# A fused attention, expert and SoLU kernel: conversions in chunks of 512 columns, and a compaction by 32 slots

## The chip, the cores and the metric

The kernel runs on one core of a Trainium2 chip. The metric is the device time of one execution in microseconds. The profile is one execution taken by the hardware profiler. Five engines run side by side, each with its own instruction queue in order: PE (matrix products; PEld is its weight load), DVE (vector), ACT (scalar, activations), POOL (vector work and indirect DMAs) and SP (it only issues DMAs).

## The reference

Three layers follow each other. The experts' layer needs a selection that is worked out from the first layer's output, and the last layer's two weight matrices come as float64.

```python
# 1 local attention: chunks of 32 queries, 16 left, 8 right, 8 memory keys
scores = scale * (q_c @ k_full.T); a = softmax(scores); out = a @ v_full
x = out.reshape(3072, 512)
# 2 experts, each takes 384 tokens; pairs are taken in order of logit
logits = x @ w_gate                       # 3072 x 8
for idx in np.argsort(-logits.flatten()):
    tok, e = idx // 8, idx % 8
    if assigned[tok] >= 0 or counts[e] >= 384: continue
    assigned[tok] = e; counts[e] += 1
x[mask_e] = np.maximum(x[mask_e] @ w1[e], 0) @ w2[e]
# 3 SoLU: w_in 512 x 1024 and w_out 1024 x 512 are float64
h = x @ w_in
solu = h * softmax(h)
ln = (solu - mean) / sqrt(var + 1e-6) * g_ln
return ln @ w_out
```

## The kernel before, in words

**Attention** (`attention`, from line 61) works through 24 blocks of 128 tokens. For one block the tiles are `kd`, `qt`, `vd` (inputs), `s` (scores), `p` (softmax), `t`/`pt` (transposed), `o`, and `xs` (the block's output, also written to `x_dram`). `xtp`, `xt`, `g` and `L` are the transposed output and the gate's logits. SP's queue issues all input loads in the order of the program.

**Route** (line 520) finds in eight rounds which expert is full next and which 384 tokens it takes. A round is a search for a threshold (tiles `ge`, `some`, `sat`, `base`), a prefix sum that gives each taken token a slot (`sl`, with `s` as the 0/1 mark of being taken), and `compact` (line 762), which turns slots into a list of tokens `idx` of 128 partitions x 3. It does so by one-hot matrices and matmuls: `ohl` is a one-hot of the slot's low bits, `rhs` holds, by the slot's high bits, the token's number, and the PE product `r` sums it up in the slots' order. Round 0 runs before the first expert, round r+1 beside stage r; it then removes the taken tokens (`gone`, `left`, `el`, `L`) and begins the next search.

**Experts** (line 806) has eight stages. A stage is `g12` (two products of 96 matmuls 128x384 each: `h` from `xh`, `xl` and `w1h`, `w1l`, then `y` from `hh`, `hl` and `w2h`, `w2l`) and two kinds of units: `g3` (`h2 = y . in`, 24 matmuls 128x512 for each of three token tiles) and `g4` (`o = l . out`, as many, for the stage before). All products are of three terms: every operand is split in a high and a low part. The tokens' rows are gathered on POOL (`xg<-x_dram,idx`), transposed on PE (`tp`) and split (`xh` on ACT, `xl` on DVE); the weights come as `raw<-in_w_dram,iw` on POOL and are split too (`w1h` on ACT, `w1l` on DVE). Results leave by an indirect DMA on POOL (`out_dram<-ob,idx`).

**Fixed** (line 410) turns the float64 matrices `win` and `wout` into pairs `in_h`, `in_l` and `out_h`, `out_l`, in chunks of `CHUNK` columns, beside all this. One chunk (line 442) is a load `raw` on SP, `v<-raw` on ACT, then on DVE the sign `e<-raw`, `v<-v,e`, the exponent `e<-v`, and `e<-raw,e`; then one or two additions on POOL, `in_h` or `out_h` on ACT, and `in_l` on POOL or `out_l` mostly on DVE. Fourteen of `win`'s 16 chunks are converted beside the attention, `wout`'s beside stages 0 and 1.

**The order.** Every instruction goes through `Timed` (line 386), and so all rows of the profile carry line 398; work is told apart by the names of tiles. `Pace` (line 238) keeps a modelled clock per engine. Jobs (generators) stand beside the main program; at each `tick` a job whose rank is within `limit` and whose condition is met emits its next instructions. Conversions have rank 3 and are spaced by `EVERY_A` and `EVERY_OUT`; where a matmul needs a chunk that is not yet there, `need` (line 506) ticks until it is. All this happens when the program is built; on the chip each engine runs its queue in the order so written:

```python
            if job[2] <= self.limit and job[0] <= self.now and (
                    job[1] is None or self.clk[job[1]] <= (self.now + self.rush if self.late() else
                                                         min(self.now + self.spare, self.soon()))):
```

## Time and profile before

| | us |
|---|---|
| median of 3 runs | 793.64 |
| the runs | 793.40, 793.64, 796.08 |
| profiled execution, its own time | 792.05 |
| its span | 790.3 |
| PE busy (share of the span) | 717.0 (91%) |
| DVE busy | 550.4 (70%) |
| ACT busy | 340.9 (43%) |
| POOL busy | 207.4 (26%) |

The span is the time from the first to the last instruction that the profiler saw; the profiled execution's own time is 1.75 us longer. PE is busy nine tenths of the span, and so time can be lost or won in two kinds of place: where PE has no work to do, and where PE's own work grows or shrinks. Along the span the attention part ends at about 117 us, the selection of round 0 at 145 us, and the first expert's matmuls begin at 153.28 us.

### The profile page before, as it was taken

Reading aid. Unit: us, or ns where it says so; the run is one execution under the profiler, and the core shown is the slowest. Engines: PE = TensorE matmul, PEld = TensorE weight load, DVE = VectorE, ACT = ScalarE, POOL = GpSimd, SP = SyncE. Lnnn points to the kernel's source line nnn. Section 1 sums busy time; section 2 is a strip of 40 time slices with the busy share of each in tenths; the row PEclk is TensorE's granted clock in tenths of the full one; section 3 lists DMA queues with packets and bytes.
Section 4 is the critical chain, followed back from the end, with each engine's and each line's share of the span. In section 5 each row is a group of like instructions: output and inputs, shape, how many; then the busy total and the mean of one; then the engine's idle time right before and its main releaser. Section 6 shows DMA issues by size and latency. Waiting matters only on the chain.

```text
span 790.3 us, 14784 instructions
## 1 busy us (share of the span) xinstructions
PE 717.0 (91%) x5728; PEld 619.6 (78%) x5728; DVE 550.4 (70%) x1536; ACT 340.9 (43%) x680; POOL 207.4 (26%) x288
## 2 busy tenths in 40 slices
PE   6988963699999949999999999999999999999993
PEld 5766653688789737998899889888988898899883
DVE  7787967699999974993798389838973952563150
ACT  1566630243574443431653174227324642463170
POOL 4344520631621342003300520052014211400121
PEclk7999995699999978999999999999999999999997
DMA  7999891720620340102600340053006110600100
GB/s 248 336 331 337 292 349 56 231 85 29 219 87 27 100 141 30 64 1 81 213 0 1 128 165 1 1 177 118 1 14 210 70 41 27 209 19 0 41 15 27
DMA packets 32326, 89.37 MB, mean 113 GB/s; under 512 B 4480, under 2 KB 4608, under 8 KB 32256
## 3 DMA queue, kind: packets, MB, share of 16 engines
q0 software_dynamic: 13056, 46.14, 17.2%
q1 hardware_dynamic: 19200, 42.29, 15.6%
q8 instruction: 45, 0.74, 0.4%
q14 instruction: 25, 0.20, 0.1%
HBM read 75.83 MB, written 12.58 MB: 112 GB/s over the span
## 4 chain that ended last, share of the span: by engine, by line
PE 69%; DVE 19%; issue 4%; POOL 3%; ACT 2%; DMA 2%; POOLq 0%; DVEq 0%
PE h L398 30%; PE y L398 17%; PE o L398 15%; DVE e L398 4%; PE tp L398 4%; PE r L398 3%; DVE sum L398 2%; DVE p L398 2%; DVE mx L398 2%; DVE v L398 1%; DMA xg<-x_dram,idx 1%; ACT p L398 1%; DVE ge L398 1%; DVE nm L398 1%; DMA raw<-in_win_dram 1%
## 5 line engine op out<-in xcount | busy, mean ns | idle before, releaser
L398 PE MATMUL y<-hh,w2h 128*128 128x384 f32 x256 | 91.7, 358 | 5.4 <-DVE e L398 5.4
L398 POOL DMA_INDIRECT out_dram<-ob,idx x24 | 26.1, 1089 | 265.6 <-ACT ob L398 223.4
L398 PE MATMUL y<-hl,w2h 128*128 128x384 f32 x256 | 88.9, 347 | 0.1
L398 PE MATMUL o<-out_h,lh 128*128 128x512 f32 x192 | 78.4, 409 | 11.2 <-ACT out_h L398 11.2
L398 PE MATMUL y<-hh,w2l 128*128 128x384 f32 x256 | 87.4, 341 | 0.0
L398 POOL DMA_INDIRECT raw<-in_w_dram,iw x64 | 62.6, 978 | 73.4 <-DVE w1l L398 27.9
L398 PE MATMUL o<-out_l,lh 128*128 128x512 f32 x192 | 76.6, 399 | 1.2 <-DVE out_l L398 1.2
L398 PE MATMUL h<-in_h,yh 128*128 128x512 f32 x192 | 76.7, 399 | 0.0
L398 PE MATMUL h<-in_l,yh 128*128 128x512 f32 x192 | 76.4, 398 | 0.0
L398 PE MATMUL o<-out_h,ll 128*128 128x512 f32 x192 | 76.4, 398 | 0.0
L398 DVE TENSOR_REDUCE nm<-h 128x1 f32<-128x512 f32 x48 | 33.0, 688 | 61.9 <-PE h L398 61.5
L398 PE MATMUL h<-in_h,yl 128*128 128x512 f32 x192 | 75.8, 395 | 0.0
L398 ACT ACTIVATE hh<-h 128x384 fp32r<-128x384 f32 x64 | 31.4, 490 | 81.0 <-PE h L398 71.2
L398 PE MATMUL h<-xh,w1h 128*128 128x384 f32 x256 | 58.3, 344 | 0.7 <-ACT xh L398 0.7
L398 ACT CAST w2h<-raw 128x512 fp32r<-128x512 f32 x64 | 39.5, 619 | 44.8 <-PE y L398 44.8
L398 PE MATMUL h<-xh,w1l 128*128 128x384 f32 x256 | 58.7, 346 | 0.0
L398 PE MATMUL h<-xl,w1h 128*128 128x384 f32 x256 | 56.9, 343 | 0.0
L398 PEld LDWEIGHTS y<-hh,w2h 128*128 128x128 f32 x256 | 48.2, 188 | 7.2 <-DVE e L398 6.8
L398 DVE TENSOR_TENSOR xl<-tp,xh 128x512 fp32r<-128x512 f32 x24 | 16.6, 691 | 50.0 <-ACT xh L398 50.0
L398 PEld LDWEIGHTS o<-out_h,lh 128*128 128x128 f32 x192 | 36.7, 191 | 18.5 <-ACT out_h L398 11.9
L398 ACT ACTIVATE ob<-o,k 128x512 f32<-128x512 f32 x24 | 16.5, 688 | 79.5 <-PE o L398 76.8
L398 DVE TENSOR_TENSOR w2l<-raw,w2h 128x512 fp32r<-128x512 f32 x64 | 44.3, 694 | 7.8 <-ACT w2h L398 7.8
(192 smaller groups left out, 1694.1 us busy)
## 6 DMA issues: line engine op xcount, KB each, us to landing
vd<-in_vx_dram SPq DMA_DIRECT2D x48, 256.0 KB, 4.9
kd<-in_kx_dram SPq DMA_DIRECT2D x48, 176.0 KB, 4.8
qt<-in_q_dram SPq DMA_DIRECT2D x24, 256.0 KB, 4.7
x_dram<-xs SPq DMA_DIRECT2D x6, 1024.0 KB, 10.4
raw<-in_win_dram SPq DMA_DIRECT2D x16, 256.0 KB, 5.0
raw<-in_wout_dram SPq DMA_DIRECT2D x16, 256.0 KB, 2.7
raw<-in_w_dram,iw POOLq DMA_INDIRECT x64, 5.5
xg<-x_dram,idx POOLq DMA_INDIRECT x24, 3.7
```

The lines of the kernel that those rows point to most:

```text
L398: return fn(*args, **kw)
```

## The change

- Conversions go in chunks of 512 columns, half as many; the intervals in `EVERY_A`, `EVERY_OUT` and `DUE_OUT` are doubled, and `raw`, `v`, `e` have two buffers each, not three. The sign is read from the dense `v` that ACT wrote, not from every second word of `raw`, so it now waits for ACT.
- From the end of round 0's searches until the first expert's rows are split, jobs of rank 3 are held (`limit = 2`). The first split of `w1` for the first expert is written after the gather.
- `compact` takes the slot as 32a+b: a one-hot of b with 32 columns (two pieces of 128x384 where there were four of 128x768), `rhs` with 12 columns for a and for each of two numbers, and 24 matmuls in which four column tiles of PE take turns. The result is cast to `cc`, four more matmuls with `rep` sum the four tiles and place them on partitions, and `tok` and `idx` follow.
- `junk` shares a ring with the output tile `ob`; some constants share work tiles.

```diff
...
-EVERY_OUT = 3.5
+EVERY_OUT = 7.0
-CHUNKS_A = 14
+CHUNKS_A = 7
-EVERY_A = 4.4
+EVERY_A = 8.8
-DUE_OUT = 5.42
+DUE_OUT = 10.84
...
-    CHUNK = 256
+    CHUNK = 512
...
-            yield from self.take("raw", 3)
+            yield from self.take("raw", 2)
             while self.hold:
                 yield 0.0
-            r = self.tmp.tile([128, C, 2], I32, tag="raw", name="raw", bufs=3)
+            r = self.tmp.tile([128, C, 2], I32, tag="raw", name="raw", bufs=2)
...
-            yield from self.take("v", 3)
-            v = self.tmp.tile([128, C], F32, tag="v", name="v", bufs=3)
-            e = self.tmp.tile([128, C], F32, tag="e", name="e", bufs=3)
+            yield from self.take("v", 2)
+            v = self.tmp.tile([128, C], F32, tag="v", name="v", bufs=2)
+            e = self.tmp.tile([128, C], F32, tag="e", name="e", bufs=2)
             vi, ei, top = v.bitcast(I32), e.bitcast(I32), r[:, :, 1]
             nc.scalar.activation(v, top.bitcast(F32), AF.Copy, scale=2.0 ** -112)
+            yield "act"
             yield "spare", "dve"
-            V.tensor_scalar(ei, top, -0x80000000, None, op0=ALU.bitwise_and)
-            yield "act"
+            V.tensor_scalar(ei, vi, -0x80000000, None, op0=ALU.bitwise_and)
             yield "spare", "dve"
             V.scalar_tensor_tensor(vi, vi, 3, ei, op0=ALU.logical_shift_left, op1=ALU.bitwise_or)
...
+        self.col = col
+        self.cnum = iota(k.tile([128, NT], F32, name="cnum"), [[1, NT]], 0, 0)
+        self.atab = iota(k.tile([128, CAP // 32], F32, name="atab"), [[32, CAP // 32]], 32, 0)
+        self.rep = k.tile([128, 32], BF, name="rep")
+        with nc.allow_low_precision(reason="0 or 1"):
+            V.tensor_reduce(self.rep, ident.rearrange("p (j b) -> p b j", b=32), axis=AX.X, op=ALU.add)
...
                 yield from self.search(lo, oh, zero, r, r + .5)
+                if not r:
+                    self.beside.limit = 2
...
-        V.tensor_scalar(low, sl, 127, None, op0=ALU.bitwise_and)
-        b = self.t("b", [NT, TT])
-        V.tensor_scalar(b[:, :, 2], sl, 256.0, None, op0=ALU.is_ge)
-        V.tensor_scalar(b[:, :, 0], sl, 128.0, None, op0=ALU.is_lt)
-        yield "spare", "dve"
-        cc = self.t("cc", [2 * TT])
-        rhs = self.t("rhs", [NT, 2, TT], BF)
-        half, part = NT // 2, NT // 4
-        for c0 in (0, half):
-            ohl = []
-            for c1 in (c0, c0 + part):
-                o = self.w.tile([128, part, 128], BF, tag="ohl", name="ohl", bufs=2)
-                V.tensor_tensor(o, self.row[:, None, :].to_broadcast([128, part, 128]),
-                                low[:, c1:c1 + part, None].to_broadcast([128, part, 128]), op=ALU.is_equal)
-                ohl.append(o)
-                if c1 == 0:
-                    V.scalar_tensor_tensor(b[:, :, 1], b[:, :, 0], -1.0, b[:, :, 2], op0=ALU.mult, op1=ALU.subtract)
-                    V.tensor_scalar(b[:, :, 1], b[:, :, 1], 1.0, None, op0=ALU.add)
-                    V.tensor_tensor(b, b, s1[:, :, None].to_broadcast([128, NT, TT]), op=ALU.mult)
-                    for a in range(2):
-                        V.tensor_tensor(rhs[:, :, a], b, self.cp[:, :, a:a + 1].to_broadcast([128, NT, TT]),
-                                        op=ALU.mult)
-                yield 0.0
+        V.tensor_scalar(low, sl, 31, None, op0=ALU.bitwise_and)
+        am = self.t("am", [NT])
+        V.scalar_tensor_tensor(am, sl, 32.0, low, op0=ALU.add, op1=ALU.subtract)
+        V.tensor_tensor(am, am, s1, op=ALU.mult)
+        yield idle
+        rhs = self.t("rhs", [NT, 2, A], BF)
+        V.tensor_tensor(rhs[:, :, 1], self.atab[:, None, :].to_broadcast([128, NT, A]),
+                        am[:, :, None].to_broadcast([128, NT, A]), op=ALU.is_equal)
+        yield idle
+        V.tensor_tensor(rhs[:, :, 0], rhs[:, :, 1], self.cnum[:, :, None].to_broadcast([128, NT, A]), op=ALU.mult)
+        yield idle
+        V.tensor_scalar(rhs[:, :, 1], rhs[:, :, 1], self.col, None, op0=ALU.mult)
+        ohl, part = [], NT // 2
+        for c in (0, part):
+            yield idle
+            o = self.w.tile([128, part, 32], BF, tag="ohl", name="ohl", bufs=2)
+            V.tensor_tensor(o, self.row[:, None, 0:32].to_broadcast([128, part, 32]),
+                            low[:, c:c + part, None].to_broadcast([128, part, 32]), op=ALU.is_equal)
+            ohl.append(o)
+        if r:
             yield "dve"
-            p = yield from self.take()
-            for c in range(half):
-                T.matmul(p[:, 0:2 * TT], ohl[c // part][:, c % part],
-                         rhs[:, c0 + c].rearrange("p a t -> p (a t)"), start=c == 0, stop=c == half - 1)
-            yield "pe"
-            if c0 == 0:
-                V.tensor_copy(cc, p[:, 0:2 * TT])
-            else:
-                V.tensor_tensor(cc, cc, p[:, 0:2 * TT], op=ALU.add)
-            self.held = False
+        p = yield from self.take()
+        for c in range(NT):
+            j = c % 4
+            T.matmul(p[32 * j:32 * j + 32, 0:2 * A], ohl[c // part][:, c % part],
+                     rhs[:, c].rearrange("p w a -> p (w a)"), start=c < 4, stop=c >= NT - 4,
+                     tile_position=(0, 32 * j), skip_group_check=True)
+        yield "pe"
+        cc = self.t("cc", [2, TT, 4], BF)
+        V.tensor_copy(cc.rearrange("p w t j -> p (w t j)"), p[:, 0:2 * A])
+        self.held = False
+        yield "dve"
+        p = yield from self.take()
+        for j in range(4):
+            T.matmul(p[32 * j:32 * j + 32, 0:2 * TT], self.rep, cc[:, :, :, j], start=True, stop=True,
+                     tile_position=(0, 32 * j), skip_group_check=True)
+        yield "pe"
+        tok = self.t("tok", [TT])
+        V.tensor_scalar(tok, p[:, 0:TT], 128.0, None, op0=ALU.mult)
         idx = self.k.tile([128, TT], I32, name=f"idx{r}")
-        V.scalar_tensor_tensor(idx, cc[:, 0:TT], 128.0, cc[:, TT:2 * TT], op0=ALU.mult, op1=ALU.add)
+        V.tensor_tensor(idx, tok, p[:, TT:2 * TT], op=ALU.add)
...
-                self.fixed.need(0, self.beside, {4 * dt + 2 * half, 4 * dt + 2 * half + 1})
+                self.fixed.need(0, self.beside, {2 * dt + half})
...
-        junk = self.wk.tile([128, DFF], BF, tag="junk", name="junk", bufs=1)
-        A.activation(junk, e, AF.Square, accum_out=sq[:, t:t + 1])
+        junk = self.wk.tile([128, DM], F32, tag="ob", name="junk", bufs=2)
+        A.activation(junk.bitcast(BF), e, AF.Square, accum_out=sq[:, t:t + 1])
...
-            self.fixed.need(1, self.beside, {2 * f, 2 * f + 1})
+            self.fixed.need(1, self.beside, {f})
...
-        self.beside.add(self.fixed.all(0, self.beside, 1.0, CHUNKS_A, 16))
+        self.beside.add(self.fixed.all(0, self.beside, 1.0, CHUNKS_A, 8))
         while 0 not in self.iw:
             tick()
         self.load_w(0, range(2))
-        self.split_w(0, 0, (1,))
         self.fixed.hold = True
         while 0 not in self.idx:
             tick()
...
         self.gather(0)
         self.load_w(0, (2,))
         self.fixed.hold = False
-        self.split_w(0, 1, (1,))
+        for f in range(2):
+            self.split_w(0, f, (1,))
...
-        self.beside.add(self.fixed.all(1, self.beside, EVERY_OUT, 0, 16))
+        self.beside.add(self.fixed.all(1, self.beside, EVERY_OUT, 0, 8))
         start = self.beside.now
-        self.beside.late = lambda: 16 - len(self.fixed.left[1]) < (self.beside.now - start - DUE_FROM) / DUE_OUT - 1
+        self.beside.late = lambda: 8 - len(self.fixed.left[1]) < (self.beside.now - start - DUE_FROM) / DUE_OUT - 0.5
...
```

The changed order, at the two places that matter below. First POOL in stage 1, where the rows of `x` for round 2 are gathered (`xg`), before the change; `v<-v,e` and `out_l` are steps of `wout`'s chunks, `na` to `k` are a norm of the last layer, and `raw` is a load of expert weights:

```order
99 L398 DMA raw_4299<-in_w_dram,iw_4188 128x1024
100 L398 DMA xg<-x_dram,idx_4370 128x512 x3
101 L398 TENSOR_TENSOR na<-s 128x3
102 L398 TENSOR_SCALAR na<-na 128x3
103 L398 TENSOR_TENSOR nv<-na 128x3
104 L398 TENSOR_TENSOR nv<-nv,q 128x3
105 L398 TENSOR_SCALAR nv<-nv 128x3
106 L398 TENSOR_TENSOR k<-nv,power 128x3
107 L398 TENSOR_TENSOR v<-v,e 128x256 x3
108 L398 TENSOR_TENSOR out_l<-v,out_h 128x256
109 L398 TENSOR_TENSOR v<-v,e 128x256
```

and POOL at the same place after it:

```order
73 L398 TENSOR_TENSOR k<-nv,power 128x3
74 L398 TENSOR_TENSOR v<-v,e 128x512 x2
75 L398 DMA raw_4127<-in_w_dram,iw_4029 128x1024
76 L398 DMA raw_4129<-in_w_dram,iw_4029 128x1024
77 L398 DMA raw_4131<-in_w_dram,iw_4029 128x1024
78 L398 DMA raw_4133<-in_w_dram,iw_4029 128x1024
79 L398 DMA raw_4135<-in_w_dram,iw_4029 128x1024
80 L398 DMA raw_4137<-in_w_dram,iw_4029 128x1024
81 L398 DMA xg<-x_dram,idx_4209 128x512 x3
82 L398 MEMSET spacer 1x1
83 L398 DMA out_dram<-ob,idx_2415 3072x512
```

Four additions of chunks stood behind the gather, the first three right behind the norm; now the last two stand ahead of the weight loads and the gather, and none comes after.

Second, DVE from the compaction of round 0 to the first expert, before:

```order
281 L398 TENSOR_TENSOR ohl<-row,low 128x768 x2
282 L398 TENSOR_TENSOR w1l<-raw_2421,w1h 128x512
283 L398 TENSOR_TENSOR cc<-cc,r 128x6
284 L398 SCALAR_TENSOR_TENSOR idx_2510<-cc 128x3
285 L398 SCALAR_TENSOR_TENSOR v<-v,e 128x256
286 L398 TENSOR_SCALAR e<-raw 128x256
287 L398 TENSOR_TENSOR xl<-tp,xh 128x4x128 x3
288 L398 TENSOR_TENSOR w1l<-raw_2421,w1h 128x512
289 L398 TENSOR_TENSOR w2l<-raw_2423,w2h 128x512 x2
290 L398 TENSOR_SCALAR gone<-s_2447 128x24
291 L398 TENSOR_TENSOR left<-left,es 128x8
```

and after, where the rows left out between go on from `gone` in the order of the kernel before:

```order
254 L398 TENSOR_TENSOR ohl<-row,low 128x384 x2
255 L398 CAST cc<-r 128x24
256 L398 TENSOR_SCALAR tok<-r 128x3
257 L398 TENSOR_TENSOR idx_2415<-tok,r 128x3
258 L398 TENSOR_TENSOR xl<-tp,xh 128x4x128 x3
...
266 L398 TENSOR_SCALAR ki<-m 128x24
267 L398 TENSOR_TENSOR ki<-ki,m 128x24
268 L398 SCALAR_TENSOR_TENSOR ge<-ki,zero,jtab 128x360
269 L398 TENSOR_TENSOR w1l<-raw_2342,w1h 128x512 x2
270 L398 TENSOR_TENSOR w2l<-raw_2344,w2h 128x512 x2
```

The first expert's `w1l` and `w2l` stood ahead of the removal of the taken tokens; now they stand behind it and behind the first comparison `ge` of the next search. No step of a conversion stands between any more.

## Rows read from the trace of the kernel before

**Rows 1.** Page, the chain that ended last: shares of the span by engine.
```profile
PE 69%; DVE 19%; issue 4%; POOL 3%; ACT 2%; DMA 2%; POOLq 0%; DVEq 0%
```

**Rows 2.** Windows: us, busy (count) PE PEld DVE ACT POOL, PEclk, DMA share, GB/s.
```profile
0.00:100.77 100.77, 83.95 (x1761) 65.10 (x1762) 81.36 (x190) 53.35 (x109) 45.78 (x60) 0.95 0.89 306
259.60:313.22 53.62, 41.23 (x189) 31.19 (x189) 37.99 (x116) 22.05 (x46) 19.05 (x27) 0.84 0.29 99
428.67:464.14 35.47, 35.47 (x181) 28.57 (x181) 19.16 (x53) 11.65 (x23) 14.31 (x16) 1.00 0.40 140
283.64:303.58 19.94, 8.56 (x23) 6.10 (x23) 10.32 (x31) 6.99 (x13) 9.76 (x17) 0.57 0.17 54
```

**Rows 3.** Timeline, PE in stage 1: start, us, work, idle before and releaser.
```profile
293.32 0.80 PE L398 MATMUL o<-out_h,lh 128*128 128x512 f32 x1 [9.60 <-ACT out_h L398]
...
297.94 0.80 PE L398 MATMUL o<-out_h,lh 128*128 128x512 f32 x1 [1.57 <-ACT out_h L398]
```

**Rows 4.** Timeline, POOL in the same stretch.
```profile
285.02 0.96 POOL L398 DMA_INDIRECT xg<-x_dram,idx  x1 [6.75 <-DVE L L398]
...
291.07 2.13 POOL L398 TENSOR_TENSOR v<-v,e 128x256 f32<-128x256 f32 x3
```

**Rows 5.** Groups of DVE by form: busy us, mean ns, idle before.
```profile
L398 DVE SCALAR_TENSOR_TENSOR e<-h,e 128x512 f32<-128x512 f32 x48 | 31.8, 688 | 7.5 <-ACT e L398 7.5
...
L398 DVE SCALAR_TENSOR_TENSOR e<-raw,e 128x256 f32<-128x256 uint32 x32 | 16.4, 511 | 0.5
L398 DVE SCALAR_TENSOR_TENSOR v<-v,e 128x256 int32<-128x256 int32 x32 | 16.3, 514 | 0.1
...
L398 DVE TENSOR_SCALAR e<-raw 128x256 int32<-128x256 int32 x32 | 13.3, 441 | 5.4 <-DMA raw<-in_win_dram 2.8 <-POOL v L398 2.6
...
L398 DVE TENSOR_SCALAR e<-v 128x256 int32<-128x256 int32 x32 | 10.5, 328 | 0.4
```

**Rows 6.** Timeline, DVE, a chunk step in stage 1.
```profile
286.46 0.43 DVE L398 SCALAR_TENSOR_TENSOR e<-raw,e 128x256 f32<-128x256 uint32 x1
```

**Rows 7.** Timeline, DVE, a chunk step of the attention part.
```profile
74.48 0.29 DVE L398 TENSOR_SCALAR e<-raw 128x256 int32<-128x256 int32 x1 [2.76 <-DMA raw<-in_win_dram]
```

**Rows 8.** Timeline, end of the attention part, PE and then DVE.
```profile
110.11 0.66 PE L398 MATMUL xtp<-ident,xs 128*128 128x128 f32 x4
...
112.66 0.68 DVE L398 COPY xt<-xtp 128x512 f32<-128x512 f32 x1
```

**Rows 9.** Timeline, DVE, compaction of round 0 and the selection behind it.
```profile
137.88 0.18 DVE L398 TENSOR_SCALAR low<-sl 128x24 int32<-128x24 int32 x1
...
138.21 0.94 DVE L398 TENSOR_TENSOR ohl<-row,low 128x768 bf16<-128x768 bf16 x1
...
145.44 0.16 DVE L398 SCALAR_TENSOR_TENSOR idx<-cc 128x3 int32<-128x3 f32 x1
...
155.67 0.30 DVE L398 TENSOR_SCALAR gone<-s 128x24 f32<-128x24 f32 x1
...
157.88 0.59 DVE L398 SCALAR_TENSOR_TENSOR ge<-ki,zero,jtab 128x360 bf16<-128x360 uint16 x1
```

**Rows 10.** Timeline, PE, the first expert's second group of matmuls.
```profile
154.66 1.48 PE L398 MATMUL h<-xh,w1l 128*128 128x384 f32 x4
```

**Rows 11.** Timeline, PE, transposes and compaction matmuls, each with its follower.
```profile
95.91 0.66 PE L398 MATMUL t<-ident,p 128*128 128x128 f32 x4
96.50 0.75 PE L398 MATMUL o<-vd,pt 128*32 128x128 f32 x20
...
196.01 0.46 PE L398 MATMUL r<-rhs,ohl 128*128 128x6 bf16 x12
196.33 0.42 PE L398 MATMUL y<-hl,w2h 128*128 128x384 f32 x1
...
753.32 0.60 PE L398 MATMUL tp<-ident,e 128*128 128x128 f32 x4
753.68 0.48 PE L398 MATMUL h<-in_h,yh 128*128 128x512 f32 x1
```

More of the change, by code (lines that the diff above doesn't have):

```diff
@@ L309, in cost @@
             return n / (480 if op == "tensor_tensor" else 960) + 0.15
-        t = (0.108 if op == "transpose" else 0.06 * n / 128 if kw.get("tile_position") else
+        t = (0.108 if op == "transpose" else max(0.03, 0.06 * n / 128) if kw.get("tile_position") else
              max(0.025, n / 2400 + 0.003))
@@ L473, in chunk @@
         else:
-            yield from self.take("v", 3)
-            v = self.tmp.tile([128, C], F32, tag="v", name="v", bufs=3)
+            yield from self.take("v", 2)
+            v = self.tmp.tile([128, C], F32, tag="v", name="v", bufs=2)
             nc.sync.dma_start(v, src[:, n * C:n * C + C])
@@ L532, in __init__, with consts @@
         self.held, self.stage = False, 0
-    def consts(self):
+    def consts(self, ident):
         nc, k = self.nc, self.k
@@ L551, in consts @@
             V.tensor_scalar(self.jtab[:, i], self.jtab[:, 3], float(16 ** (3 - i)), None, op0=ALU.mult)
-        off = iota(self.t("off", [8, E]), [[-15, 8], [0, E]], 0, 1)
+        off = iota(self.w.tile([128, 8, E], F32, tag="oh", name="off"), [[-15, 8], [0, E]], 0, 1)
         self.own = k.tile([128, 8, E], F16, name="own")
-        up = self.t("up", [8, E])
+        up = self.w.tile([128, 8, E], F32, tag="rhs", name="up")
         V.tensor_scalar(up, off, 0.0, None, op0=ALU.is_ge)
@@ L765, in compact @@
         V, T = nc.vector, nc.tensor
+        A, idle = CAP // 32, ("spare", "dve") if r else 0.0
         low = self.t("low", [NT], I32)
-        V.tensor_scalar(low, sl, 127, None, op0=ALU.bitwise_and)
-        b = self.t("b", [NT, TT])
-        V.tensor_scalar(b[:, :, 2], sl, 256.0, None, op0=ALU.is_ge)
-        V.tensor_scalar(b[:, :, 0], sl, 128.0, None, op0=ALU.is_lt)
-        yield "spare", "dve"
-        cc = self.t("cc", [2 * TT])
-        rhs = self.t("rhs", [NT, 2, TT], BF)
-        half, part = NT // 2, NT // 4
@@ L803, in compact @@
+        self.held = False
         self.idx[r] = idx
@@ L1191, in step @@
         beside.tick()
-    attention(nc, tc, q, kx, vx, wg, ident, x_dram, L, route.consts, step)
+    attention(nc, tc, q, kx, vx, wg, ident, x_dram, L, lambda: route.consts(ident), step)
     route.open_psum(ctx)
```

5 lines of the change are left out of this document (1 added, 4 removed).

## The prediction

> **What bounds the kernel now.** I read the chain of waits first: it gives 69% of the span to PE and 19% to DVE, 3% to POOL and 2% to DMA [rows 1]. So time is mostly PE's own work, and the second candidate is DVE where PE waits for it. Then I put stages side by side with the windows. The last part of stage 1, from the first `h2` matmul to the next stage's first `h`, takes 53.62 us, and the same 144 matmuls in stage 3 take 35.47 with PE busy all the time [rows 2]. Stage 1 thus loses 53.62 - 35.47 = 18.15 us. The reader is to see where: in 283.64 to 303.58 PE is busy for 8.56 us only, and the granted clock has a mean of 0.57 [rows 2]. PE's timeline names the wait: 9.60 us for `out_h`, and 1.57 for it again a little later [rows 3]. ACT's copy to `out_h` needs `v<-v,e` of POOL, and POOL's timeline shows why that is late: POOL waited 6.75 us for the selection with its gather of `x` for round 2 at 285.02, and three additions of chunks, queued behind it and behind a norm, began at 291.07 [rows 4]. The third place is the front. In the first 100.77 us DVE is busy for 81.36 us and the DMA engines for a share of 0.89 [rows 2]; one chunk step there waited 2.76 us for `raw` [rows 7].
>
> All sums below are made on the profiled execution's 792.05 us (span 790.3). The median of the runs shown, 793.64, is 1.59 us above it.
>
> **Stage 1's stall: -15.5 us.** In the new order of POOL the last two additions of `wout`'s chunks stand ahead of the weight loads and the gather, so no matmul `o` can wait for the selection through them. What goes: 9.60 + 1.57 us of idle PE, and the low clock. The 8.56 us of PE work in that window ran at about half speed, so half of it, 4.3 us, comes back. 9.60 + 1.57 + 4.3 = 15.5. Bounds: 9.6 (the one wait alone) and 18.2 (all that stage 1 loses). What is late next is the gathered `x` itself: stage 1 would now end at 313.2 - 15.5 = 297.7 us, and the gather's three issues would still be out by about 289 (285.02 and three times 0.96 with small gaps), so its rows have some 9 us to land, be transposed and split. I take it as enough; a rival below does not.
>
> **Attention: -3.2 us.** Two chunks of 256 columns become one of 512. Four DVE steps each: 511 + 514 + 441 + 328 ns = 1.79 us per chunk now, 14 chunks in this part, so 25.1 of DVE's 81.4 busy us [rows 2, 5]. A step with fixed time f costs 0.43 us at 256 columns [rows 6] and 0.688 at 512 (the same kind of operation, `e<-h,e`) [rows 5], so f = 2 x 0.43 - 0.69 = 0.17 us is saved once per pair: 4 steps x 7 pairs x 0.17 = 4.8 us. The sign from the dense tile costs 0.328 where the strided read cost 0.441: 14 x 0.11 = 1.6 us. Together 6.4 us of DVE. How much of it is on the path? DMA moves the same bytes at a share of 0.89, so at one end nothing is gained; at the other all 6.4, since the chain has 19% on DVE and 2% on DMA. I take the middle, 3.2. The sign now waits for ACT; other DVE work stands between, so I cost it at nothing; without that cover it is one ACT copy per chunk. With two `raw` buffers a load is issued only when the chunk before last is through with its last DVE step; its cost is the slower rival.
>
> **End of the attention part: -1.8 us.** The last-but-one transposes `xtp` ended at 110.11 + 0.66 = 110.77, and DVE's copy `xt` began at 112.66, with steps of chunks queued ahead of it [rows 8]. In the new order none is: 112.66 - 110.77 = 1.9, less 0.1 for the signal, 1.8. Bounds 0 (something else late there, as the last `o`) and 4 (each of the two last copies gains as much).
>
> **Compaction of round 0: -3.1 us.** Only here does PE wait for it. Before: 137.88 to 145.44 + 0.16, 7.7 us [rows 9]. After: three short steps at 0.18 = 0.5; three steps for `rhs` on 288 columns, the nearest row being `ge` with 0.59 us for 360 columns, so 0.47 each = 1.4; two one-hots of half of the old one's 768 columns, 0.94 / 2 = 0.5 each, 1.0; `cc`, `tok` and `idx` at 0.16 = 0.5; and two trips to PE and back at an estimated 0.6 = 1.2. Sum 4.6, gain 3.1; bounds 2.5 (the `rhs` steps at 0.69 like a step of 512 columns) and 4.5 (the trips at 0.2 each and `rhs` at 0.3).
>
> **First expert's weights: +2.8 us.** What the front gains there is given back by the order on DVE: `w1l` now stands behind `gone` to `ge`. These run from 155.67 to 157.88 + 0.59 = 158.47, 2.8 us [rows 9], and the four matmuls `h<-xh,w1l` that began at 154.66 [rows 10] with only four others ahead of them wait for as long. Bounds 0 (the selection's steps fall in DVE's gaps between the three `xl`) and 4.5 (the clock falls too, as it did in stage 1).
>
> **Compactions in rounds 1 to 7: +4.0 us.** These stand in PE's dense stretches, so what PE spends is lost. Before, a group of 12 matmuls takes 196.33 - 196.01 = 0.32 us until the next `y`, 27 ns each, two groups a round: 0.64 [rows 11]. After, 24 + 4 matmuls at 27 ns = 0.75, if column tiles don't overlap. And PE changes between full and column-tiled use twice a round. Its price shows in the attention: four transposes next to tiled matmuls take 96.50 - 95.91 = 0.59 us, four next to full ones 753.68 - 753.32 = 0.36 [rows 11], so 0.23 per change there and back. 0.75 + 2 x 0.23 - 0.64 = 0.57 a round, times 7 = 4.0. Bounds: all tiles overlap and the change is free, 28 x 27 / 4 = 0.19, 7 x (0.19 - 0.64) = -3.2; and a change at twice the price, 7 x 1.03 = +7.2.
>
> The rows show 0.23 us per change. The Trainium skill's page "TensorEngine Tiling (Array Packing)", section Key Properties, says that changing the tiling mode drains the engine; the two rows agree in sign, and it speaks against this part of the change. The same page, section Theoretical Speedup, gives up to 4x for a small side of at most 32; by that alone the 28 matmuls would be the 0.19 us of the lower bound.
>
> DVE's relief in these rounds (two one-hots of 384 columns for four of 768, about 3 us a round) I cost at nothing: in stage 3's last part DVE is busy for 19.16 of 35.47 us and PE never waits [rows 2]. `junk` in the output's ring may wait for an output DMA; it is an ACT step with a stage's matmuls before its use, so nothing either.
>
> **Sum.** -15.5 - 3.2 - 1.8 - 3.1 + 2.8 + 4.0 = -16.8, and 792.05 - 16.8 = 775.3 us.
>
> **Rivals.**
> - *A new wait takes part of the stall's place.* The gather for round 2 still hangs on the selection, whose DVE steps now share the queue with chunk steps of twice the length. For: POOL waited 6.75 us for it [rows 4]. Against: those 9 us of room. If `x` comes some 4 us too late, PE idles 4 us, and by the stall's ratio (15.5 lost for 11.2 idle) loses 5.5: 780.8.
> - *The front gives nothing.* The attention is bound by DMA and the copies at its end by something else. For: the share of 0.89 and the wait for `raw` [rows 2, 7]. Against: the chain's 2% on DMA [rows 1]. Without 3.2 and 1.8: 780.3.
> - *Column tiles overlap and changes are cheap.* For: the compaction's matmuls are independent in fours. Against: 0.59 against 0.36 us [rows 11]. The rounds then cost -1.5 in place of +4.0 (the middle between -3.2 and no change): 769.8.
> - *Slower.* With two `raw` buffers SP's queue stops at a load of `raw` until a chunk is through, and the loads of `kd`, `qt`, `vd` behind it are late; the attention waits for each. Five of seven loads in the attention have to wait for a buffer. It decides from the point where the other 16.8 + 3.2 = 20 us are eaten: 4 us in each of the five. For: DMA-bound, few buffers. Against: inputs are loaded five blocks ahead, about 20 us at 100.77 / 24 = 4.2 us a block. At 5 us each: 792.05 - 20 + 25 + 3.2 in lost relief, about 800.
>
> **How the numbers follow.** Forecast 0.50, new wait 0.13, front nothing 0.17, overlap 0.15, slower 0.05. What a measurement of this kernel can tell from no change is about 0.5%, 4 us. The forecast's own range is 769 to 781; with the neighbours and the bounds of stall (-18.2 to -9.6), front and rounds I give 766 to 784, which leaves out the slower case and the sums in which several bounds fall on one side. The first four cases are all more than 8 us below 793.64; only several high bounds together (stall 9.6, front 0, rounds +7.2) come within 4 us, 0.03, and 0.01 of the slower case. Faster 0.92, same 0.04, slower 0.04.
>
> **What would show it.** In the profile after: no wait of PE for `out_h` or `out_l` over 2 us in stage 1, and its last part near 37 us; the attention's last block begun some 3 us before 100.77; 4.6 us from `low` to `idx` in round 0; `h<-xh,w1l` of the first expert waiting for DVE's `w1l` for about 3 us; and about 1.2 us of PE per compaction in later rounds. It is wrong if stage 1 keeps over 8 us of idle PE, whoever is waited for, or if PE waits for `kd` or `vd` in the attention.

## The result and the profile after

The changed kernel takes 784.46 us (median of 4 runs, 784.17 to 785.33) where the kernel before, run beside it, takes 794.86 (793.40 to 797.55). The ratio is 0.9872 with a 95% interval of 0.9849 to 0.9895: faster by 1.3%, 10.4 us. Forecast were 775.3 us and a range of 766 to 784. The direction held; the gain of 16.8 us that the forecast added up became 10.4, and the time lies 0.46 us outside the range.

The profiled execution after took 785.33 us (span 783.6), so the two profiles are 6.7 us apart, not 10.4: that of before lies 2.8 us below its median, that of after 0.9 above. The accounts below are of the 6.7 us, with one profile for each kernel. The windows of the changed kernel, with the columns of [rows 2]: stage 0 (`g12`, then `g3`), stage 1 (`g12`, then `g3` and `g4`), and the first 10 us of stage 0 again.

```profile
153.40:206.17 52.77, 47.75 (x423) 41.31 (x424) 47.59 (x126) 20.14 (x37) 13.47 (x10) 0.90 0.23 72
206.17:224.30 18.13, 18.13 (x85) 14.71 (x85) 17.07 (x29) 11.23 (x23) 12.18 (x11) 1.00 0.82 269
224.30:269.22 44.92, 41.17 (x245) 38.56 (x243) 39.09 (x109) 24.16 (x48) 6.14 (x9) 0.96 0.10 33
269.22:305.57 36.35, 36.35 (x193) 28.28 (x193) 27.01 (x88) 18.05 (x36) 14.38 (x21) 1.00 0.36 124
153.40:163.40 10.00, 7.59 (x59) 5.99 (x60) 7.97 (x23) 3.62 (x7) 2.41 (x2) 0.54 0.39 131
```

The same stretches of the kernel before, as far as [rows 2] do not have them:

```profile
153.28:199.38 46.10, 45.47 (x408) 40.55 (x408) 42.99 (x127) 18.80 (x40) 10.36 (x11) 0.96 0.23 71
199.38:218.54 19.16, 18.74 (x97) 14.85 (x97) 17.31 (x42) 11.25 (x26) 12.47 (x14) 1.00 0.72 250
218.54:259.60 41.06, 39.56 (x244) 36.91 (x243) 39.23 (x114) 24.45 (x50) 7.21 (x11) 1.00 0.14 44
153.28:163.28 10.00, 10.00 (x80) 9.20 (x81) 9.40 (x28) 4.69 (x11) 2.08 (x2) 0.83 0.49 162
```

The reader is to see that stage 1's last part went from 53.62 to 36.35 us with PE busy throughout, and that the two first parts (46.10 to 52.77, 41.06 to 44.92) grew. The attention, which ends here with the start of its last `mx`, grew too. As a table, each part from one start time to the next:

| part | before | after | change | forecast |
|---|---|---|---|---|
| attention, to the start of the last `mx` | 100.77 | 105.15 | +4.4 | -3.2 |
| from there to the first `m` of round 0 | 15.43 | 13.58 | -1.9 | -1.8 |
| searches, `m` to `low` | 21.68 | 21.05 | -0.6 | 0 |
| compaction, `low` to the end of `idx` | 7.72 | 5.26 | -2.5 | -3.1 |
| `idx` to the first `h` | 7.68 | 8.36 | +0.7 | 0 |
| stage 0, first part | 46.10 | 52.77 | +6.7 | +2.8 |
| stage 0, `g3` | 19.16 | 18.13 | -1.0 | +0.6 |
| stage 1, first part | 41.06 | 44.92 | +3.9 | 0 |
| stage 1, `g3` and `g4` | 53.62 | 36.35 | -17.3 | -14.9 |
| stages 2 to 7 and the end | 477.08 | 478.03 | +1.0 | +2.8 |

(The forecast's +0.57 a compaction stands in the last two rows and in stage 0's `g3`.) The first two rows belong together. By its last `mx` the changed kernel has converted six chunks of 512 columns, the kernel before ten of 256, and it does three more between its last `mx` and the first `m`. So a part of the +4.4 is work that stood later before; both rows together are +2.5 where -5.0 was forecast. DVE's group for one step of a chunk in the kernel before, up to 101 us (that of the changed kernel stands in experiment 1):

```profile
L398 DVE SCALAR_TENSOR_TENSOR v<-v,e 128x256 int32<-128x256 int32 x10 | 5.6, 566 | 0.0
```

**Attention, after.** DVE's timeline around 64 us, where a step of 256 columns took 0.43 us [rows 6], and POOL's at the same time:

```profile
64.18 1.46 DVE L398 TENSOR_SCALAR e<-v 128x512 int32<-128x512 int32 x1
65.67 1.65 DVE L398 SCALAR_TENSOR_TENSOR v<-v,e 128x512 int32<-128x512 int32 x1
```

```profile
64.08 1.28 POOL L398 TENSOR_TENSOR v<-v,in_h 128x512 f32<-128x512 f32 x1
65.44 1.34 POOL L398 TENSOR_TENSOR in_l<-v,e 128x512 fp32r<-128x512 f32 x1
```

Both DVE steps begin beside a POOL addition and end after it; where POOL is idle, `e<-v` takes 0.42 us (106.56 us in the same trace) and `v<-v,e` 0.69.

**Compaction and the first expert, after.** DVE against [rows 9], then PE against [rows 10]:

```profile
139.78 0.18 DVE L398 TENSOR_SCALAR low<-sl 128x24 int32<-128x24 int32 x1
...
144.20 0.18 DVE L398 CAST cc<-r 128x24 bf16<-128x24 f32 x1 [1.49 <-PE r L398]
...
144.88 0.16 DVE L398 TENSOR_TENSOR idx<-tok,r 128x3 int32<-128x3 f32 x1
...
153.47 0.17 DVE L398 TENSOR_SCALAR gone<-s 128x24 f32<-128x24 f32 x1
...
155.56 0.59 DVE L398 SCALAR_TENSOR_TENSOR ge<-ki,zero,jtab 128x360 bf16<-128x360 uint16 x1
156.08 1.28 DVE L398 TENSOR_TENSOR w1l<-raw,w1h 128x512 fp32r<-128x512 f32 x2
```

```profile
153.40 1.00 PE L398 MATMUL h<-xh,w1h 128*128 128x384 f32 x4 [1.19 <-ACT w1h L398]
156.81 0.69 PE L398 MATMUL h<-xh,w1l 128*128 128x384 f32 x1 [2.41 <-DVE w1l L398]
```

`w1l` waits behind `gone` to `ge`, as forecast; but PE also waits for `w1h`, and the two waits are followed by a low clock: 0.54 of full speed over the first 10 us where before it was 0.83.

**A compaction in a dense stretch.** PE in stage 3, after, and then before, against [rows 11]:

```profile
426.18 0.39 PE L398 MATMUL o<-out_h,ll 128*128 128x512 f32 x1
426.50 0.32 PE L398 MATMUL r<-rhs,ohl 128*32 128x24 bf16 x24
426.75 0.50 PE L398 MATMUL o<-out_h,lh 128*128 128x512 f32 x1
427.09 0.40 PE L398 MATMUL o<-out_l,lh 128*128 128x512 f32 x1
427.42 0.19 PE L398 MATMUL r<-cc,rep 128*32 128x6 bf16 x4
427.54 0.50 PE L398 MATMUL o<-out_h,ll 128*128 128x512 f32 x1
...
432.49 0.66 PE L398 MATMUL tp<-ident,xg 128*128 128x128 f32 x4 [0.35 <-DMA xg<-x_dram,idx]
```

```profile
434.35 0.39 PE L398 MATMUL o<-out_l,lh 128*128 128x512 f32 x1
434.58 0.45 PE L398 MATMUL r<-rhs,ohl 128*128 128x6 bf16 x12
434.89 0.48 PE L398 MATMUL o<-out_h,ll 128*128 128x512 f32 x1
435.21 0.39 PE L398 MATMUL o<-out_h,lh 128*128 128x512 f32 x1
```

24 column-tiled matmuls take 0.25 us to the next start, less than 12 full ones (0.31). The first `o` behind either takes 0.31 to 0.34 in place of 0.23. What the tiled groups have besides is a price ahead of them: the `o` at 426.18 and that at 427.09 take 0.32 and 0.33 to the next start, while the `o` at 434.35, ahead of an old group, takes its usual 0.23. It is so ahead of all 14 tiled groups of rounds 1 to 7, with 0.09 to 0.10 us more each time. A round so costs 0.25 + 0.12 + 2 x 0.09 + 2 x 0.11 = 0.77 us, where two old groups cost 2 x (0.31 + 0.1) = 0.82. What makes the stage 0.46 us longer all the same (35.93 after, 35.47 before) is the wait of 0.35 for `xg` at 432.49, which the kernel before does not have. Where the new compaction runs without that wait (experiment 6, the new compaction alone), this part of stages 3 to 5 takes 35.36 to 35.38 us, against 35.40 to 35.48 before.

### The profile page after: what moved, and what is told of

Its sections match the earlier page's. It is cut to its first block, busy times and chain, and to the rows that moved or that the text cites. A ratio compares the mean times of both kernels' runs of the same rounds, so it can differ in the third digit from the quotient of the medians.

```text
span 783.6 us, 14636 instructions
## 1 busy us (share of the span) xinstructions
PE 715.6 (91%) x5760; PEld 616.5 (79%) x5760; DVE 528.2 (67%) x1434; ACT 335.9 (43%) x646; POOL 199.2 (25%) x263
## 3 DMA queue, kind: packets, MB, share of 16 engines
q0 software_dynamic: 13056, 46.14, 17.3%
## 4 chain that ended last, share of the span: by engine, by line
PE 72%; DVE 17%; issue 3%; ACT 3%; DMA 2%; POOL 1%; POOLq 0%; DVEq 0%; ACTq 0%
PE h L398 32%; PE y L398 16%; PE o L398 15%; PE tp L398 4%; PE r L398 3%; DVE e L398 3%; DVE sum L398 2%; DMA xg<-x_dram,idx 2%; DVE p L398 2%; DVE mx L398 1%; DVE ge L398 1%; ACT p L398 1%; DVE w1l L398 1%; PE xtp L398 1%; PE g L398 1%
## 5 line engine op out<-in xcount | busy, mean ns | idle before, releaser
L398 POOL DMA_INDIRECT out_dram<-ob,idx x24 | 24.3, 1014 | 227.4 <-ACT ob L398 227.0
L398 PEld LDWEIGHTS h<-xh,w1l 128*128 128x128 f32 x256 | 46.6, 195 | 3.3 <-DVE w1l L398 3.2
L398 PEld LDWEIGHTS y<-hl,w2h 128*128 128x128 f32 x256 | 48.5, 189 | 0.2
```

The source lines that it names most:

```text
L398: return fn(*args, **kw)
```

## The experiments

Times are medians; the kernel before, run beside them, had 793.15 to 794.38 us. "Stages" are stage 0 and 1 as first part + `g3`, first part + rest.

**1. Additions of win's chunks left out, in both kernels.** In the chunk code of win, with the planner's charge kept:

```diff
-            G.tensor_tensor(v if wide else lo, v, hi.bitcast(F32), op=ALU.subtract)
...
-                G.tensor_tensor(lo, v, e, op=ALU.add)
...
+            raw_g.tensor_tensor(v[:, 0:1], v[:, 0:1], hi[:, 0:1].bitcast(F32), op=ALU.subtract)
+            raw_g.tensor_tensor(lo[:, 0:1], v[:, 0:1], e[:, 0:1], op=ALU.add)
```

> The changed kernel with the two POOL additions of each of win's chunks cut to one column (in_l is left at zero but for those columns); the order of all instructions in the attention part is kept. Theory: in the attention DVE's steps of 512 columns stand still while a POOL addition of 512 columns runs (rows of 1.46 and 1.65 us where 0.42 and 0.69 are usual); then the last mx starts at 99 to 101 us, not at 105.15, and the mean of e<-v falls from 638 to about 430 ns. Rival 1: the attention waits for loads, since raw has two buffers and 512 KB a load; then the last mx stays at 104 to 106. Rival 2: the longer steps themselves are late at the next block; then it comes down by 1 to 2 us only.

> The kernel before with the two POOL additions of each of win's chunks cut to one column (in_l is left at zero but for those columns). Theory: POOL's additions of 256 columns hold DVE as well, for less time each; the last mx comes from 100.8 to 98 to 100 us, a smaller gain than the 4.4 us with 512 columns. Rival: below a certain length they cost nothing; then 100.5 to 101.

Groups of DVE in the attention part, mean ns after the comma: first the changed kernel up to 106 us, then without the additions, up to 101 us.

```profile
L398 DVE TENSOR_SCALAR e<-v 128x512 int32<-128x512 int32 x12 | 8.0, 675 | 0.1
L398 DVE SCALAR_TENSOR_TENSOR v<-v,e 128x512 int32<-128x512 int32 x6 | 5.8, 974 | 0.1
```

```profile
L398 DVE TENSOR_SCALAR e<-v 128x512 int32<-128x512 int32 x12 | 4.9, 416 | 0.1
L398 DVE SCALAR_TENSOR_TENSOR v<-v,e 128x512 int32<-128x512 int32 x6 | 4.9, 815 | 0.1
```

The start of the first and the last `mx`, from the view of that tile: the kernel before, the changed kernel, and in the same order both without the additions.

```profile
L398 DVE TENSOR_REDUCE mx<-s x24: 639/656/692, 11.6 to 100.8; 128x8 f32<-128x512 f32 x24
```

```profile
L398 DVE TENSOR_REDUCE mx<-s x24: 639/641/692, 11.8 to 105.2; 128x8 f32<-128x512 f32 x24
```

```profile
L398 DVE TENSOR_REDUCE mx<-s x24: 639/678/694, 13.6 to 101.0; 128x8 f32<-128x512 f32 x24
```

```profile
L398 DVE TENSOR_REDUCE mx<-s x24: 639/641/694, 13.8 to 100.8; 128x8 f32<-128x512 f32 x24
```

Both edits fill in_l with zeros first, by which the attention begins 2 us later, while its loads go on (DMA share 0.97 to 1.00 from 10 to 14 us in all four). The last `mx` of the changed kernel comes from 105.2 to 100.8 all the same, as expected (779.13 us, a single execution). That of the kernel before goes from 100.8 to 101.0 (790.52 us, a single execution too), which is what the rival said and not the theory. Counted from the first `mx` to the last it is 89.2 and 93.4 us with the additions, and 87.4 and 87.0 without. So additions of 256 columns cost between nothing and 1.8 us and those of 512 between 4.4 and 6.4, for nearly the same work on POOL; and without them the changed DVE steps, though shorter in sum, win 0.4 us at most. The profiles scatter: four with the attention of the kernel before (itself and experiments 5, 6 and 7) have the last `mx` at 99.6 to 101.5, five with the changed one at 103.2 to 105.2. Against the middle one of the five, 103.7, the price of the 512 columns is 2.9 to 4.9 us. The Trainium skill's page "SBUF — State Buffer", section "SBUF: two separate sides", says that DVE in certain modes, or with two inputs in SBUF, and GpSimd (POOL) share a port that one instruction holds to its end, the other blocking fully. The rows at 64 us and the fall of `e<-v` from 675 to 416 ns, and of `v<-v,e` from 974 to 815, agree.

**2. Halves, and fewer bytes.** The additions of the changed kernel in two pieces of 256 columns; and, in the kernel before, every second chunk of win in the attention without a load (in_h and in_l hold wrong columns there):

```diff
-            G.tensor_tensor(v if wide else lo, v, hi.bitcast(F32), op=ALU.subtract)
-            if wide:
-                G.tensor_tensor(lo, v, e, op=ALU.add)
+            for q in (slice(0, C // 2), slice(C // 2, C)):
+                G.tensor_tensor(v[:, q], v[:, q], hi[:, q].bitcast(F32), op=ALU.subtract)
+                G.tensor_tensor(lo[:, q], v[:, q], e[:, q], op=ALU.add)
```

```diff
+            if m == 0 and n % 2 and n < CHUNKS_A and self.last is not None:
+                r = self.last
...
```

> The changed kernel with each POOL addition of a win chunk cut in two of 256 columns, all work kept. Theory: what holds the attention up is the length of one POOL addition (a DVE step waits for the end of the one that runs); the last mx comes from 103.2 to 105.2 (four kernels with the same attention part) to 101 to 102.5. Rival: the total of POOL's additions counts, or the longer DVE steps; then no change, 103 or more.

> The kernel before, in whose attention part every second chunk of win is converted from the chunk loaded before it (no load of its own; in_h and in_l hold the wrong columns there); DVE's steps in the attention part keep their order. Seven loads of 256 KB, 1.8 MB, fall out of about 32 MB. Theory: the attention part is bound by DMA (share 0.97 between 20 and 80 us at 336 GB/s); the last mx comes from 100.8 to about 95 to 97 us. Rival: DVE's work bounds it; no change (100 to 101.5).

Halves: the last `mx` at 102.5 (781.65 us, a single execution), and at 102.9 in experiment 9, where the five kernels with the changed attention part have 103.2 (twice), 103.7, 104.0 and 105.2. The means are 1.1 us apart and the nearest two profiles 0.3: the length of one addition is at most a part of the price. Fewer bytes: 99.2 against 100.8 (792.01 us, a single execution), and against 99.6 to 101.5 in the four profiles with this attention: 0.4 to 2.4 us earlier, not the 4 to 6 of a DMA bound, and hardly clear of the scatter. What sets the 100.8 us of the kernel before stays open.

**3. The first expert's first split put back.** In the changed kernel:

```diff
         self.load_w(0, range(2))
+        self.split_w(0, 0, (1,))
         self.fixed.hold = True
...
-        for f in range(2):
-            self.split_w(0, f, (1,))
+        self.split_w(0, 1, (1,))
```

> The changed kernel with the first expert's first split of w1 put back ahead of the hold, as before the change; its w1l then stands ahead of gone to ge on DVE. Theory: stage 0's first part (52.8 us from the first h to the first h2, 46.1 before) loses its waits for w1h and w1l and the long half clock, and comes to 46 to 48.5; the time is 4 to 6 us below the changed kernel's 784.5. Rival: the conversion steps of 512 columns in the search of round 1 hold it up; then the first part stays over 50 and the time within 2 us.

```profile
151.90:198.97 47.07, 44.00 (x396) 38.73 (x397) 44.14 (x114) 20.30 (x37) 12.10 (x8) 1.00 0.26 80
151.90:161.90 10.00, 8.91 (x87) 7.87 (x87) 9.30 (x26) 5.27 (x10) 2.08 (x2) 1.00 0.49 162
```

779.84 us, ratio to before 0.9833 (0.9787 to 0.9879), 4.6 us below the changed kernel, as expected. The first part fell from 52.77 to 47.07 us, its first 10 us at a clock of 1.00; with halved additions on both sides (experiment 2 and experiment 9) it falls from 51.88 to 47.06. So the place of that one split was worth 4.8 to 5.7 us, about twice the 2.8 that its queue on DVE explains. An estimate puts the rest down to the clock: in the changed kernel's first 10 us PE's 7.59 us of work ran at 0.54, so about 3.5 us of it were lost, and with the wait of 2.41 that makes 5.9. But experiment 9 has the same 47.06 us with a clock of 0.83 over its first 10 us, so how much of it is the clock's is not shown.

**4. The old compaction in the changed kernel.** `compact` and its constants as before, `b` in a shared tile.

> The changed kernel with the old compaction (one-hot of 128 columns, two groups of 12 matmuls 128 wide). Theory: PE's cost per compaction in rounds 1 to 7 is nearly the same for both (stages 2 to 7 are only 0.95 us longer after the change), and round 0's is 2.5 us longer with the old one; the time is 1 to 4 us above the changed kernel's. Rival, the prediction's: changes between full and column-tiled use cost 0.57 us a round; the old one then gives 4 us back and takes 2.5, so it is 1 to 2 us faster than the changed kernel.

787.43 us, ratio 0.9908 (0.9873 to 0.9943): 3.0 us above the changed kernel, within the 1 to 4 expected, but not for the reason given. Round 0's compaction takes 6.19 us, only 0.9 more than the new one's 5.26. Stages 52.32 + 20.28, 46.89 + 37.82, which is 157.3 us against 152.2: it is there that the old compaction is longer, by 5 us in one profile each. Stages 3 to 5 are at 35.4 again. And the stall of stage 1 does not come back (37.82), so the new compaction is not what ended it.

**5. Gather moved behind the chunks.** In the kernel before:

```diff
-        if r in self.idx and (r, "x") not in self.done:
+        if r in self.idx and (r, "x") not in self.done and (r != 2 or not self.fixed.left[1]):
```

> The kernel before with one edit: the gather of x for round 2 is written only when all of wout's chunks are converted, so that POOL's additions no longer stand behind it. Theory: the stall of stage 1 goes by order alone; the last part of stage 1 falls from 53.6 to 36 to 39 us and the time by 14 to 18 us, to 776 to 780, better than the changed kernel. Rival: the wait moves to the rows of x or to the chunks' own steps on DVE; then 5 to 10 us are won and the next stage begins with a wait for x.

792.35 us, ratio 0.9984 (0.9959 to 1.0008): no change. The last part of stage 1 is still 51.13 us, 2.5 less than before. PE, POOL with its additions now ahead of the gather, and DVE with the last step of the first of these chunks:

```profile
292.79 0.80 PE L398 MATMUL o<-out_h,lh 128*128 128x512 f32 x1 [6.82 <-ACT out_h L398]
```

```profile
290.54 1.45 POOL L398 TENSOR_TENSOR v<-v,e 128x256 f32<-128x256 f32 x2
...
297.21 1.10 POOL L398 DMA_INDIRECT xg<-x_dram,idx  x1 [0.16 <-issue]
```

```profile
288.71 0.43 DVE L398 SCALAR_TENSOR_TENSOR e<-raw,e 128x256 f32<-128x256 uint32 x1
```

The gather in POOL's queue was not the main cause. DVE is through with this chunk at 289.14, when PE has already waited for 3.2 us; POOL's addition, now behind the norm alone, begins 1.4 us later, and 2.2 us after that PE goes on. In the kernel before the same step of DVE ended at 286.89 [rows 6], also 3.2 us into the wait, but the addition began at 291.07 [rows 4], 4.2 us later. So POOL's queue made 4.2 of the 9.60 us; this order gets 2.8 of them back, and PE's next wait for `out_h` is 2.89 us for 1.57. What both orders share is DVE: in the kernel before it does not begin these chunks until the selection of round 2 is over:

```profile
284.34 0.17 DVE L398 TENSOR_SCALAR el<-es 128x8 f32<-128x8 bf16 x1
...
285.07 0.69 DVE L398 TENSOR_SCALAR e<-raw 128x256 int32<-128x256 int32 x3
...
288.75 0.43 DVE L398 SCALAR_TENSOR_TENSOR e<-raw,e 128x256 f32<-128x256 uint32 x1
```

After the change the last chunk's `e<-raw,e` stands at 272.02 and the compaction's `low` at 282.99.

**6. Is DVE's work as a whole the bound?** That was my second theory. The new compaction alone in the kernel before, chunks of 256 with three buffers in the changed kernel, and `out_l` taken from DVE (early split kept):

```diff
-POOL_OUT = 4
+POOL_OUT = 1
```

> The kernel before with the new compaction alone (chunks of 256, three buffers, no hold, the old places of the splits). Theory: stages 0 and 1 are bound by DVE as a whole (137.5 us of DVE work in 159.9 us before, 130.8 in 152.2 after), and the stall is where the debt is paid; two new compactions there take about 5 us of work off DVE, so the two stages together fall by 4 to 7 us from 159.9, round 0 gains 2.5, later rounds lose 0.4 each: 785 to 788 us. Rival, the prediction's: the stall hangs on the order of POOL's queue alone; it is then still over 15 us, and the time falls by 0 to 3 us, or it goes as a whole, and the time falls by 15.

> The changed kernel with chunks of 256 columns, three buffers, sign from raw and the old intervals; new compaction, hold and late split of w1 kept. Theory: without POOL additions of 512 columns the attention's last mx comes back to 100 to 102 us; DVE has about 3 us more work in stages 0 and 1, and these come to 153 to 158 us; the time is 781 to 786. Rival: the longer chunk is what ends the stall; then the last part of stage 1 is over 48 us again and the time over 788.

> The changed kernel with the early split, and out_l of all of wout's chunks made by ACT and POOL, none by DVE (six steps of 0.86 us leave DVE). Theory: stages 0 and 1 are bound by DVE's work; they fall together by 3 to 5 us from the 146 us of the run with the early split alone. Rival 1: they are bound by the order of steps; no change within 1 us. Rival 2: POOL's additions of 512 columns hold DVE for as long as they save; no change or 1 to 3 us longer.

It fell three times. New compaction alone: 802.96 us, ratio 1.0121 (1.0085 to 1.0156), slower, where 785 to 788 was expected, though DVE has less to do; stages 48.59 + 18.88, 44.26 + 57.79, PE waiting for `out_h` for 12.30 and 5.08 us. Chunks of 256: 791.82, ratio 0.9970 (0.9953 to 0.9987), stages 50.64 + 18.12, 41.86 + 48.22. The stall is back, as this run's rival had it: with experiment 4 this says that the part of the change that touches the chunks ended it. `out_l` on POOL: 786.24, ratio 0.9913 (0.9886 to 0.9940), stages 50.89 + 19.44, 46.02 + 36.83, 7 us more than with the early split alone; DVE was busy there for 112.4 us in the three parts other than stage 0's `g3`, against 111.4, though six steps had left it. Why it is so much longer is not shown; the expectation's second rival had 1 to 3 us.

**7. Order alone.** In the kernel before:

```diff
-RUSH = 0.57
+RUSH = 1.0
```

> The kernel before with one number changed: RUSH 0.57 to 1.0, by which late conversions of wout may stand further ahead on DVE; in DVE's queue no chunk step is left behind the selection of round 2 (four are in the kernel before). Theory: the stall of stage 1 is made by those four chunks' DVE steps and not by POOL's queue; the last part of stage 1 falls from 53.6 to 36 to 39 us, 2 to 6 us come back as waits in the first parts of stages 0 and 1, and the time falls by 10 to 15 us to 779 to 785. Rival: DVE has too much work in stages 0 and 1 as a whole; the wait then only moves to an earlier place and the time falls by under 4 us.

```profile
218.42:263.62 45.20, 40.72 (x241) 38.38 (x240) 39.72 (x115) 24.73 (x51) 8.65 (x13) 0.96 0.18 58
263.62:303.08 39.46, 37.63 (x196) 28.77 (x195) 32.30 (x105) 18.94 (x40) 16.95 (x23) 1.00 0.35 114
```

785.33 us, ratio 0.9889 (0.9852 to 0.9926): 7.8 us faster, where 10 to 15 were expected. One number of the planner, with nothing else of the change, takes 14.2 us out of the last part and gives 4.1 back in the first, where `y` now waits twice for 1.70 us for DVE's `e`. Its last chunk is through at 279.29 on DVE, ahead of `low` at 281.51. The number moves the chunks' steps on every engine: POOL's last addition now begins at 279.87, ahead of its gather at 292.59. So experiments 5 and 7 together show that POOL's order alone does not end the stall and the order of the chunks' steps does; DVE's order changed with POOL's left as it was has not been run.

**8. Mixed chunks.** 256 for win, 512 for wout, early split, two buffers; then the same with RUSH 1.0 and 1.3; and the early split alone with RUSH 0.8:

```diff
...
-    CHUNK = 512
+    CHUNK = (256, 512)
...
```

> The changed kernel with chunks of 256 for win and 512 for wout, two buffers for both, and the early split of w1. Theory: the attention as with 256 columns (last mx at 100 to 102 us), stages 0 and 1 as in the run with the early split alone (about 146 us); the time is 775 to 779. Rival: with two buffers, not three, the chunks of 256 are late and the attention stays at 103 us or more; then 780 or above.

> Chunks of 256 for win and 512 for wout with the early split, as run before, and RUSH 1.0: no chunk step behind the selection of round 2 on DVE (two were). Theory: the front as in that run (first h at 146.7 us), stages 0 and 1 as in the run with the early split alone (146 us, the last part of stage 1 at 36 to 39): a span of 771 to 774, time 773 to 776, faster than both kernels. Rival: the chunks pushed ahead hold the first parts of stages 0 and 1 up by over 6 us; then 780 or above.

> The same with RUSH 1.3. Theory: the same within 3 us, since the stall goes as soon as no chunk step stands behind the selection of round 2; pushed further ahead, chunk steps cost some us in the first parts of stages 0 and 1. Rival: more push is better, the time is over 3 us below that of RUSH 1.0.

> The changed kernel with the early split and RUSH 0.8 for 0.57: late chunks of wout may stand further ahead on DVE; none stands behind the selection of round 2 in either. Theory: where no chunk step stands behind that selection RUSH has nothing to win; within 2 us of the run with the early split (779.8). Rival: stages 0 and 1 fall below 144 us and the time below 777.

Mixed: 789.91 us, ratio 0.9948 (0.9928 to 0.9968). The last `mx` is at 98.1, but with less done: 10 loads of win were issued by 106 us where the kernel before has 13. The rest went into stage 0, and the stall was back (stage 1: 43.37 + 52.67). RUSH 1.0 and 1.3: 787.02 and 786.05, last parts of 48.01 and 48.21: the expectation was wrong. No chunk step stands behind the selection any more, but one stood inside it: at RUSH 1.0 the last `out_h` came at 290.40, after PE had begun to wait. What counts is whether `out_h` is there when PE comes, not the rank in the queue. RUSH 0.8 with the early split: 779.73, as expected no different from 779.84.

**9. The best version.** Early split and halves together:

> The same halves together with the early split of w1. Theory: the last mx at 101 to 102.5 and stages 0 and 1 as in the run with the early split (146 us): 777 to 779 us, 1 to 2 us below that run. Rival: as long as that run or longer, since POOL has 7 x 2 more instructions.

775.95 us (775.18 to 776.88), ratio 0.9761 (0.9720 to 0.9801): 8.5 us below the changed kernel and 3.9 below the early split alone, where 1 to 2 were expected. The two profiles are 1.6 us apart; where the rest lies is not shown.

## Why the prediction was right or wrong

In the profiles the sum was to be -16.8 us and was -6.7. Three parts came out worse than forecast: the attention by 7.6 us, the first part of stage 0 (the first expert) by 3.9, and the first part of stage 1, which the sum left at nothing, by 3.9. The others came out some 5 us better. The step that failed most is the attention's: it priced DVE's steps one by one and gave POOL's longer additions no price. That the time lies only 0.46 us outside the range is in part luck: the +4.0 for the compactions, which is not there, made up for a part of the misses. Without it the forecast would have been 771.3.

- **Stage 1's stall, -15.5: right in size (-17.3), right only in part in its cause.** The prediction put it on POOL's queue behind the gather. Experiment 5 moved the gather away and 51.13 of 53.62 us stayed; experiment 7 changed the order of the chunks' steps alone and the stall went. POOL's queue held the three additions [rows 4] for 4.2 us of PE's wait of 9.60; the step that failed is the one that stopped there, since DVE's steps for these chunks came only behind the selection. The step "what is late next" failed too: it named only the gathered rows of `x`. The last part became 36.35 us with PE busy throughout, but stage 1's first part grew by 3.9, and by 4.1 in experiment 7, where the chunk steps had moved ahead of the selection. That they are what the first part pays for after the change too is inferred from that likeness.
- **Attention, -3.2: failed, +4.4.** Each step was costed from a row with POOL idle. The steps' number fell as forecast, but a step beside a POOL addition of twice the length takes up to 1.65 us. Without the additions (experiment 1) the last `mx` comes back to 100.8, and the shorter steps win 0.4 us at most: so the rival "the front gives nothing" held for the attention (not for its end), and the longer additions came on top. The sum also counted 14 old chunks in the first 100.77 us, where ten stand; the changed kernel converts a fifth more columns in this part.
- **End of the attention, -1.8: right,** -1.9.
- **Compaction of round 0, -3.1: nearly,** -2.5; `cc` waited 1.49 us for PE where a trip was put at 0.6. The 7.7 us of the old one hold a `w1l` and a chunk step that the order put between. With those steps held, as after the change, the old compaction takes 6.19 (experiment 4), so about 1 us of the 2.5 is the new compaction's and the rest the order's, by one profile each.
- **First expert, +2.8: mechanism right, price too low.** Experiment 3 gives 4.8 to 5.7 for it. The wait for `w1l` was 2.41; `w1h` on ACT behind three `xh` was left out, and the low clock stood only in the bound of 4.5, itself too small.
- **Compactions, +4.0: the term was wrong in size.** It took the 0.23 us between two pairs of transposes [rows 11] for the price of a change of mode there and back, and 27 ns for each tiled matmul. What runs show is about 0.09 us ahead of each tiled group and 0.01 to 0.02 more behind it than behind an old one, and 10 ns for each of the 24. So a round costs 0.77 us against 0.82, the rival of overlapping tiles was right, and a wait of 0.35 for `xg` took that back. The Trainium skill's rule that a change of tiling mode drains the engine, in the page and section that the prediction names, agrees with the 0.09 us ahead of each tiled group at 426.50 and 427.42; its price here is less than half of what the prediction took.
- **DVE's relief at nothing: right in stage 3, open in stages 0 and 1.** Experiment 4 has these two stages 5 us longer with the old compaction, experiment 6 has them 9.6 us longer with the new one alone (169.5 against 159.9). The effect hangs on the order of the rest; that it is DVE's relief is not shown.

## What to carry to other kernels

Where a wait ends at an instruction behind a queue, follow the operands back past that queue to the engine that was late first, before pricing its removal; then ask where the work that left the queue will stand. A longer piece of work on one engine has to be priced beside what shares its time: here additions of 256 columns on POOL cost the attention at most about 2 us and the same work in pieces of 512 between 3 and 6. With a planned order, one edit moves steps everywhere: the new compaction alone made the kernel slower by 1.2%, and was worth 3 us with the rest.

## What the runs showed of the hardware

A DVE step of 0.42 us took 1.46 beside POOL additions of 1.28 us. 24 column-tiled matmuls of 32 x 24 (inner size 128) inside a dense stretch took 0.25 us, 10 ns each, where 12 full ones of 6 columns took 0.31; the full matmul ahead of a tiled group took 0.09 us longer than usual. Waits of PE of 1.19 and 2.41 us at the start of stage 0 stood beside a granted clock of 0.54 over 10 us, mostly the lower of its two levels (1.2 and 2.4 GHz). With a single wait of 0.67 or 0.68 us there the clock was 0.83 (the kernel before, experiment 9) or 1.00 (experiment 3): that wait alone does not decide it.
